# Output rows in falling order: reversed through device memory, two tiles stored from another queue, and a last pair in another order (attention with an FNet mixing block, one Trainium2 core)

## The chip, the cores and the metric

The kernel runs on one core of a Trainium2 chip. The metric is the device time of one execution in microseconds. Three runs of the kernel before gave 1046.66, 1045.99 and 1046.56 us, a median of 1046.56. One further execution was recorded by the hardware profiler; all rows below come from it.

The engines have short names in the profile: PE is TensorE's matmul, PEld its weight load, DVE is VectorE, ACT is ScalarE, POOL is GpSimd, SP is SyncE. SP computes nothing here; it issues DMAs. SPq and ACTq are the queues in which SP and ScalarE issue them. An engine issues its instructions strictly in order, so a DMA that has to wait holds up everything behind it on the same engine.

## The reference

Four batches of 768 rows with 8 heads of 64 columns. A blocked-sparse attention first, then a Fourier mixing over rows and columns, a normalization, and a two-layer multiplication with a residual:

```python
# q, k, v: (4, 8, 768, 64); mask: window of blocks, first and last block, 3 sampled blocks per row block
scores = scale * np.matmul(q, k.transpose(0, 1, 3, 2))
scores = np.where(mask, scores, -1000000000.0)
attn = softmax(scores)                        # with 1e-9 added to the sum
x = np.matmul(attn, v).transpose(0, 2, 1, 3).reshape(4, 768, 512)

mixed = np.real(np.fft.fft(np.fft.fft(x, axis=1), axis=2))
u = x + mixed
un = (u - mean(u)) / np.sqrt(var(u) + 1e-06)  # over the 512 columns
out = u + np.maximum(un @ w_ch1, 0.0) @ w_ch2 # w_ch1: 512x2048, w_ch2: 2048x512
```

The output is `out`, 4 x 768 x 512 in float32.

## The kernel before, in words

**Attention.** The 32 pairs of heads and batches are worked off in slots; a slot holds a few units of scores. `s` (L583) is the matmul of scores, ScalarE and VectorE make `e` from it (L603 or L611 and L613), `o` (L657) multiplies it with the values. At the end of a pair the result `oT` is transposed by TensorE (`xt`, L680) and copied by ScalarE into the activations of its batch (`x<-xt`, L681). For some pairs of the later batches the way goes through device memory instead (`row<-oT`, L696, and `x<-row`, L700).

**The activations.** A batch has two tiles in SBUF, `xA` and `xB`, of 128 partitions x 3 x 512: six tiles of 128 rows, numbered 0 to 5. Each of the two names has two buffers, so a batch uses the buffers of the batch two before it: the first `x<-xt` of a batch waits until every output store of the batch two before has read that buffer.

**The mixer** of a batch runs beside the attention of the batch after it: a list of small steps (Fourier folds, normalization `un`, the channel layers) that a planner places into the slots. The planner keeps a modelled time for each engine (`busy`), and steps have due times. The list of matmuls is thereby fixed when the kernel is built. The normalized rows `un` of some tiles go to device memory (`far<-un`, L1020) and come back transposed (`unT<-far`, `fetch`, L1032: four DMAs for each half); the matmuls `xp`, `yp` and `z` of L1116 need them, `z` after a subtraction on VectorE (`t`, L1070). Both kinds are issued by SP.

**The output.** `channels` (L1270) makes `y` (L1281: a tile of the first layer times a chunk of `w_ch2`) and adds it to `x` in place (L1284). In the last round of a tile `store` (L1289) sends it to the output, all on SP's queue. In the first three batches the tiles of half 0 come in the order 2, 0, 1, and those of half 1 in the order 3, 4, 5. In the last batch, where no attention is left to run beside it, tiles m and m + 3 are made as a pair, with products and sums of blocks (`outputs`, `product` L1349, `plus` L1356), in the order m = 0, 1, 2; the last pair stores its four halves of 256 columns as each is done, one of them from ScalarE's queue.

**Which rows a tile holds.** The Fourier symmetry makes partitions correspond to rows in an unusual order, listed in `_ORDER` and turned into access patterns by `_rows`. Tiles 0 and 1 hold even and odd rows in two runs of 64: two DMAs of `64x512`. In tiles 2, 3 and 4 the rows *fall*: partitions 1 to 126 hold two interleaved runs of 63 descending rows, which a DMA writes with the pattern `[[row, 2], [-2 row, 63], [1, 512]]` (a `2x63x512` in what follows), and partitions 0 and 127 hold one row each, with a DMA of their own. Tile 5 has rising rows in four runs of 1, 48, 15 and 64 rows.

**Completions.** A DMA's end is counted by a semaphore. The DMAs of SP and ScalarE use eight of these in rotation, and a DMA waits until the one eight before it has landed.

**Loads on the same queue.** The blocks of k and q (`kb`, `qb`, L232) and v (`vr`, L272) of later pairs are also issued by SP.

These are the functions that the change touches, and those that call them:

Of the kernel before, what the change touches and what calls it, by code (L numbers as in the profile page):

```python
# [11 lines left out]
FP32 = mybir.dt.float32  # L12
# [5 lines left out]
ALU = mybir.AluOpType  # L18
ACT = mybir.ActivationFunctionType
# [61 lines left out]
def _rows(view, tile):  # L81

    got = []
    for t, p0, runs, jump, n, s0, step in _ORDER:
        if t != tile:
            continue
        at = view[s0:s0 + 1, :]
        row, col = list(at.ap[0])[0], list(at.ap[1])
        if jump > 0 > step:
            got.append((p0, runs * n, bass.AP(tensor=at.tensor, offset=at.offset,  # L90
                                              ap=[[jump * row, runs], [step * row, n], col])))
            continue
        for r in range(runs):
            at = view[s0 + r * jump:s0 + r * jump + 1, :]
            got.append((p0 + r * n, n, bass.AP(tensor=at.tensor, offset=at.offset,
                                               ap=[[step * row, n], col])))
    return got
# [3 lines left out]
def kernel(  # L101
# [14 lines left out]
    nc = tc.nc  # L116

    B, H, S, D = q.shape
    DM = H * D
    FF = w_ch1.shape[1]  # L120
    P = 128
# [9 lines left out]
    T = C // 2  # L131
# [55 lines left out]
    far_p = ctx.enter_context(tc.tile_pool(name="far_p", bufs=1, space=bass.MemoryType.DRAM))  # L187
    ps_s = ctx.enter_context(tc.tile_pool(name="ps_s", bufs=2, space=PSUM))
    ps_o = ctx.enter_context(tc.tile_pool(name="ps_o", bufs=1, space=PSUM))
    ps_t = ctx.enter_context(tc.tile_pool(name="ps_t", bufs=1, space=PSUM))  # L190
    ps_m = ctx.enter_context(tc.tile_pool(name="ps_m", bufs=2, space=PSUM))
# [3 lines left out]
    when = {"PE": 0.0, "ACT": 0.0, "DVE": 0.0, "POOL": 0.0}  # L195
    free = {"m": [0.0, 0.0], "t": [0.0]}

    def busy(engine, us, after=0.0):
        when[engine] = max(when[engine], after) + us
        return when[engine]  # L200
# [101 lines left out]
    def bit(n):  # L302
# [5 lines left out]
                      in_=bass.AP(tensor=_words(sampled_blocks, NB * NR), offset=0,  # L308
                                  ap=[[0, NB], [1, 2 * NB * NR]]))
# [138 lines left out]
    for w, w_sb in ((w_ch1, w1_sb), (w_ch2, w2_sb)):  # L448
        rows, cols = w.shape
        words = _words(w, rows * cols)  # L450
        for row in range(rows // P):
            for col in range(0, cols, WN):
                src = bass.AP(tensor=words, offset=2 * (row * P * cols + col),
                              ap=[[2 * cols, P], [1, 2 * WN]])
# [527 lines left out]
    z_at = [0.0, 0.0]  # L982
    rstd_at = deque()
    finished = set()
    folded = set()

    def mixer(b, xA, xB):
# [4 lines left out]
        tt = nc.vector.tensor_tensor  # L992
# [51 lines left out]
        t, s = {}, {}  # L1044
# [243 lines left out]

        def store(half, m, cols=slice(0, DM), queue=nc.sync):  # L1289
            x = (xA, xB)[half]  # L1290
            for p0, cnt, rows in _rows(out[b][:, cols], T * half + m):
                queue.dma_start(out=rows, in_=x[p0:p0 + cnt, m, cols])
            if cols.stop == DM:
                stored[half] += 1
            if stored[half] == T:
                finished.add((b, half))

        stored = [0, 0]
        last = b == B - 1
        OUT = (0, 1, 2) if last else (2, 0, 1)
        out_of = (OUT, OUT if last else (0, 1, 2))
        o_t, o_s = {}, {}
        DH = DM // 2

        def block(r, k, n):
            return w2_sb[:, 8 * r + 4 * k:8 * r + 4 * k + 4, n * DH:n * DH + DH]
# [25 lines left out]
        def outputs(r, m, after):  # L1335

            if m == OUT[0]:
                output_left(m, 1)
                output_left(m, 2)
            a11, a12, a21, a22 = (hs[g, i][:, :, m * P:(m + 1) * P]  # L1340
                                  for i in range(2) for g in range(2))
            a0, a1 = xA[:, m, 0:DH], xA[:, m, DH:DM]
            b0, b1 = xB[:, m, 0:DH], xB[:, m, DH:DM]
            rights = {j: [o_t[j, 0], o_t[j, 1]] for j in (1, 2, 3, 4)}

            def product(pool, tag, a, c):
                ps = pool.tile([P, 512], FP32, tag=tag, name="yy")[:, 0:DH]
                for k in range(4):
                    nc.tensor.matmul(ps, a[:, k, :],  # L1349
                                     c[k // 2][:, k % 2, :] if isinstance(c, list) else c[:, k, :],  # L1350
                                     start=(k == 0), stop=(k == 3))
                busy("PE", 1.75)
                return ps

            def plus(to, a, c=None):
                tt(out=to, in0=a, in1=to if c is None else c, op=ALU.add)  # L1356
                busy("DVE", 0.43)

            def ahead(j):
                if after is not None:  # L1360
                    output_left(after, j)

            ends = r == 1 and after is None
            u = sum_p.tile([P, DH], FP32, tag="oT", name="u")
            p1 = product(ps_m, "m", a11, block(r, 0, 0))
            nc.scalar.copy(out=u, in_=p1)
            plus(a0, p1)
            plus(a0, product(ps_m, "m", a12, block(r, 1, 0)))
            if ends:
                store(0, m, slice(0, DH))  # L1370
            if m == OUT[0]:
                output_left(m, 3)
                output_left(m, 4)
            plus(u, product(ps_t, "t", a21, rights[2]), u)
            plus(a1, u)
            plus(b0, product(ps_s, "s", a22, rights[4]))
            plus(u, product(ps_s, "s", o_s[m, 3], rights[3]), u)
            both = xB[:, m, :].rearrange("p (n d) -> p n d", n=2)
            tt(out=both, in0=both,
               in1=u.rearrange("p (o d) -> p o d", o=1).broadcast_to([P, 2, DH]), op=ALU.add)  # L1380
            busy("DVE", 0.7)


            if ends:
                store(1, m, slice(0, DH), nc.scalar)
            p5 = product(ps_o, "o", o_s[m, 1], rights[1])
            plus(b1, p5)
            if r == 1:
                store(1, m, slice(DH if ends else 0, DM))
            plus(a1, p5)  # L1390
            ahead(1)
            ahead(2)
            ahead(3)
            p3 = product(ps_m, "m", o_s[m, 4], block(r, 1, 1))
            plus(a1, p3)
            if r == 1:
                store(0, m, slice(DH if ends else 0, DM))
            ahead(4)

        fl = [[("tm"[h == 1 and m != 0], lambda h=h, m=m: un_flip(h, m), 0.6, 0.55, 0.0)  # L1400
# [10 lines left out]
              for m, us in (((1, 2), RIGHT), ((0,), COMBINE))]  # L1411
        le = [("d", lambda i=i: left(0, i), 0.0, 0.0, COMBINE) for i in (1, 3, 4)]
        after = ([fl[0][1], sp[1][1]] + le +
                 [fl[0][2], sp[1][2], wh[1][1], fl[0][0], sp[1][0], wh[1][2],
                  fl[1][1], fl[1][2], wh[1][0]] + ri[0] + [fl[1][0]] + ri[1])
        if not last:
# [5 lines left out]
            after = ([("-", un_back, 0.0, 0.0, 0.0)] + le +  # L1422
                     [("b", lambda i=i: right(i, 0, 1, 2), 0.0, 0.0, 1.0 if b else 1.7)
                      for i in (1, 2, 3, 4)])
# [5 lines left out]
        for r in range(0 if last else NF // 4):  # L1430
# [21 lines left out]
    needed = set()  # L1452
    state = {"paired": False, "total": None, "w": 0, "got": 0, "owed": 0.0, "ready": 0.0,
             "back": 0.0, "place": None,
             "alone": False, "drain": lambda: None}

    def channel_step():
        masks["by_pe"] = False
# [62 lines left out]
    def until(met, alone=False):  # L1521

        state["alone"] = alone
        while not met():
            if late:
                channel_step()
                soon = state.pop("soon", None)
                gap(2.0, start=soon)
            else:
                do_apart()  # L1530
        state["alone"] = False
# [24 lines left out]
    def w_loads():  # L1556
        while state["got"] < min(len(wchunks), state["w"] + len(W_ROOMS)):
            w_load(state["got"])
            state["got"] += 1

    def w_steps(sl):
        while state["w"] < min(len(wchunks), W_PACE * sl):
            w_round(state["w"])
            state["w"] += 1

    def slot(sl):
        phase, r = divmod(sl, SB)
        n, s = divmod(sl, SP)
        units = range(SLOT * sl, SLOT * sl + SLOT)
# [55 lines left out]
        if s >= ((4 if late else 5) if reuse else 3) and (n, 0) in oT_at and once(n):  # L1625
            b, j = pairs[n]
            at = oT_at[n, 0]
# [12 lines left out]
        if sl < B * SB and n % NP == 1 and s == 1:  # L1640
            b = pairs[n - 1][0]
            at = oT_at[n - 1, 1]
            if b >= 2:
                until(lambda: (b - 2, 1) in finished)
                at = when["PE"] + LEAVES
# [46 lines left out]
        while short and (not more or soon) and (  # L1692
# [5 lines left out]
            short.remove(item)  # L1698
            item[2]()
        w_loads()  # L1700
        w_steps(sl)
        table_step(sl)

# [32 lines left out]
    begin(B - 1)  # L1736
    state["drain"] = lambda: None
    until(lambda: len(finished) == 2 * B, True)
    ordered.close()

    def general():
# [4 lines left out]
        for b in range(B):  # L1748
            xs = [xp.tile([P, T, DM], FP32, tag=tag, name="x") for tag in ("xA", "xB")]
            for h in range(H):  # L1750
                qt = ld.tile([P, C, 2, D], FP32, tag="q", name="qg")
                for t in range(C):
                    for p0, cnt, rows in _rows(q[b, h], t):
                        nc.sync.dma_start(out=qt[p0:p0 + cnt, t, 0, :], in_=rows)
                nc.sync.dma_start(out=qt[:, :, 1, :],
                                  in_=k[b, h].rearrange("(p c) d -> p c d", p=P))
                vt = ldv.tile([P, C, D], FP32, tag="v", name="vg")
                nc.sync.dma_start(out=vt, in_=v[b, h].rearrange("(p c) d -> p c d", p=P))
                for half in range(2):
# [4 lines left out]
                    sl = slice(half * HS, (half + 1) * HS)  # L1764
# [3 lines left out]
                op = ps_o.tile([P, C, D], FP32, tag="o", name="og")  # L1768
# [32 lines left out]
                step[1]()  # L1801
            for fn, _ in rest:
                fn()

    with tc.If(over > 0):
        general()
# [37 lines left out]
```

## Time and profile before

| | us |
|---|---|
| median of three runs | 1046.56 |
| the profiled execution | 1045.29 |
| its span, first to last instruction | 1043.6 |
| TensorE (PE) busy | 1018.6 |
| VectorE busy | 683.2 |
| ScalarE busy | 359.3 |
| mean granted TensorE clock, of full speed | 0.994 |
| last matmul begins | 1035.48 |
| last sum (DVE, L1356) ends | 1035.92 |
| last output store lands | 1041.70 |

The profiled execution's time stands 1.7 us over its span. A row such as `653.32 2.93 PE L583 MATMUL s<-qT,kT 64*128 64x384 f32 x8 [4.52 <-DVE e L613]` is read thus: from 653.32 us after the span's start, for 2.93 us, PE ran eight matmuls of line 583; it had been idle for 4.52 us before, and what ended that idle time was VectorE's `e` of line 613. For a row of SPq or ACTq the second number is the time in which the queue issued the DMAs, waits between them included; when their data landed is read from the events of their semaphores, and the number of such events tells on how many DMA engines a transfer ran.

The second batch's half 0 is stored from 633.06 us on, the first batch's from 389.61 on.

### The profile page before, as it was taken

How to read it: one execution, taken by the hardware profiler on the slowest of the kernel's cores; microseconds unless marked ns; L12 is line 12 of the kernel's file. 1: busy time of each engine (PE TensorE's matmuls, PEld its weight loads, DVE VectorE, ACT ScalarE, POOL GpSimd, SP SyncE). 2: the span in 40 equal slices, each digit the busy share in tenths (PEclk: the TensorE clock that was granted, in tenths of full speed). 3: DMA queues.
4: the chain of work that ended last, by engine and by line, in shares of the span. 5: the costliest groups of instructions: out<-in, count | busy, mean ns of one | idle time of the engine just before them, and what ended most of it. 6: DMA issues, size and time to landing. Idle time of an engine off the chain costs nothing.

```text
span 1043.6 us, 12498 instructions
## 1 busy us (share of the span) xinstructions
PE 1018.6 (98%) x4382; PEld 537.0 (51%) x4382; DVE 683.2 (65%) x1246; ACT 359.3 (34%) x727; POOL 257.7 (25%) x287
## 2 busy tenths in 40 slices
PE   8999999999999999999999998999999999999996
PEld 4444345435565454444535653444444764578575
DVE  6899895978745646655677367665458475674663
ACT  6998765563021012433341111253220221210210
POOL 1000173662000203545560003256540221000000
PEclk9999999999999999999999999899999999999998
DMA  7767422291000143322320005521010001000001
GB/s 213 225 190 234 99 47 46 51 153 25 1 1 20 41 58 65 73 47 45 63 46 1 1 20 101 91 48 43 17 23 8 0 1 42 20 0 1 1 19 45
DMA packets 163582, 58.06 MB, mean 56 GB/s; under 512 B 144298, under 2 KB 154296, under 8 KB 163512
## 3 DMA queue, kind: packets, MB, share of 16 engines
q1 hardware_dynamic: 162216, 56.46, 24.1%
q10 hardware_dynamic: 1264, 0.72, 0.3%
q8 instruction: 36, 0.59, 0.2%
q14 instruction: 34, 0.28, 0.1%
q0 software_dynamic: 32, 0.01, 0.0%
HBM read 43.80 MB, written 13.37 MB: 55 GB/s over the span
## 4 chain that ended last, share of the span: by engine, by line
PE 84%; DVE 8%; DMA 2%; ACT 2%; SPq 2%; issue 1%; ACTq 0%; DVEq 0%
PE y L1281 20%; PE z L1116 16%; PE s L583 11%; PE o L657 9%; PE yp L1116 8%; PE yy L1349 7%; PE xp L1116 4%; PE zp L865 2%; PE sp L728 1%; PE s L593 1%; DMA far<-un 1%; ACT e L603 1%; DVE t L1070 1%; PE yz L1224 1%; DVE acc L638 1%
## 5 line engine op out<-in xcount | busy, mean ns | idle before, releaser
L643 POOL TENSOR_TENSOR acc<-acc,e 128x384 f32<-128x384 f32 x160 | 163.4, 1054 | 126.3 <-DVE e L613 106.7
L583 PE MATMUL s<-qT,kT 64*128 64x384 f32 x768 | 154.5, 518 | 9.5 <-DVE e L613 5.4
L657 PE MATMUL o<-e,vr 128*64 128x384 f32 x768 | 141.7, 497 | 0.0
L1281 PE MATMUL y<-w_sb,hB 128*128 128x512 f32 x264 | 118.9, 601 | 0.0
L1281 PE MATMUL y<-w_sb,hA 128*128 128x512 f32 x264 | 117.1, 595 | 0.0
L613 DVE TENSOR_TENSOR e<-s,mask 128x768 f32<-128x768 f32 x86 | 78.3, 950 | 53.9 <-ACT s L611 45.9
L583 PEld LDWEIGHTS s<-qT,kT 64*128 64x128 f32 x768 | 64.4, 187 | 90.0 <-ACT e L603 22.7
L1284 DVE TENSOR_TENSOR x<-y,x 128x512 f32<-128x512 f32 x66 | 45.6, 691 | 98.3 <-PE y L1281 98.1
L611 ACT ACTIVATE s<-s 128x768 f32<-128x768 f32 x86 | 65.1, 791 | 107.3 <-PE s L583 107.2
L603 ACT ACTIVATE e<-s 128x768 f32<-128x768 f32 x106 | 81.0, 814 | 54.2 <-PE s L593 32.9
L643 POOL TENSOR_TENSOR acc<-e 128x384 f32<-128x384 f32 x42 | 48.7, 1180 | 201.5 <-ACT e L603 121.9
L1116 PE MATMUL z<-unT,t 128*128 128x384 f32 x256 | 93.1, 486 | 0.0
L657 PEld LDWEIGHTS o<-e,vr 128*64 128x64 f32 x768 | 47.9, 136 | 69.4 <-issue 67.0
L1281 PEld LDWEIGHTS y<-w_sb,hB 128*128 128x128 f32 x264 | 49.6, 192 | 62.0 <-issue 61.3
L1121 DVE TENSOR_TENSOR hA<-z,hA 128x384 f32<-128x384 f32 x64 | 35.7, 557 | 69.8 <-PE z L1116 69.7
L1281 PEld LDWEIGHTS y<-w_sb,hA 128*128 128x128 f32 x264 | 49.2, 190 | 59.5 <-issue 55.7
L1125 ACT ACTIVATE hA<-hA 128x384 f32<-128x384 f32 x64 | 33.5, 523 | 121.8 <-DVE hA L1121 121.8
L1116 PEld LDWEIGHTS z<-unT,t 128*128 128x128 f32 x256 | 48.6, 190 | 34.1 <-DVE hA L1121 0.4
L1125 ACT ACTIVATE hB<-hB 128x384 f32<-128x384 f32 x64 | 33.5, 523 | 86.0 <-DVE hB L1121 86.0
L1136 ACT COPY hA<-xp 128x384 f32<-128x384 f32 x32 | 15.3, 477 | 129.3 <-PE xp L1116 129.3
L1116 PE MATMUL z<-t,w_sb 128*128 128x384 f32 x128 | 46.7, 487 | 1.5 <-DVE t L1070 1.5
L1116 PE MATMUL xp<-unT,w_sb 128*128 128x384 f32 x128 | 47.2, 492 | 0.0
(236 smaller groups left out, 1440.4 us busy)
## 6 DMA issues: line engine op xcount, KB each, us to landing
wraw<-in_moe_w_ch_dram SPq DMA_DIRECT2D x32, 512.0 KB
vr<-in_v_dram SPq DMA_DIRECT2D x30, 192.0 KB
far<-un SPq DMA_DIRECT2D x18, 256.0 KB
unT<-far SPq DMA_DIRECT2D x24, 192.0 KB
qb<-in_q_dram SPq DMA_DIRECT2D x44, 96.0 KB
kb<-in_k_dram SPq DMA_DIRECT2D x44, 96.0 KB
out_dram<-x SPq DMA_DIRECT2D x11, 252.0 KB
out_dram<-x SPq DMA_DIRECT2D x19, 128.0 KB
```

Source lines behind the costliest of these rows:

```text
L583: nc.tensor.matmul(s[:, i, 0:HS], kT[rows, c * P:(c + 1) * P], qT[rows, queries], start=True, stop=u not in by_pe)
L603: nc.scalar.activation(out=e, in_=s[:, :, 0:HS], func=ACT.Exp, scale=scale)
L611: nc.scalar.activation(out=s[:, :, 0:HS], in_=s[:, :, 0:HS], func=ACT.Exp, scale=scale)
L613: nc.vector.tensor_tensor(out=e, in0=s[:, :, 0:HS], in1=m.broadcast_to([P, 2, HS]), op=ALU.mult)
L643: nc.gpsimd.tensor_add(out=acc[:, i, :], in0=start[:, i, :], in1=e[:, i, :])
L657: nc.tensor.matmul(o[D * i:D * i + D, :], vt[:, i, c, :], e[:, i, :], start=(c == 0), stop=(c == C - 1))
L1116: nc.tensor.matmul(to, a[:, k, :], c[:, k, :], start=(k == 0), stop=(k == ND // 2 - 1))
L1121: tt(out=to, in0=ps, in1=a, op=ALU.add)
L1125: nc.scalar.activation(out=h, in_=h, func=ACT.Relu)
L1281: nc.tensor.matmul(y, hs[0, half][:, l, m * P:(m + 1) * P], w2_sb[:, 4 * r + l, :], start=(l == 0), stop=(l == 3))
L1284: nc.vector.tensor_tensor(out=x[:, m, :], in0=y, in1=x[:, m, :], op=ALU.add)
L1349: nc.tensor.matmul(ps, a[:, k, :], c[k // 2][:, k % 2, :] if isinstance(c, list) else c[:, k, :], start=(k == 0), stop=(k == 3))
```

## The change

1. **Falling tiles through device memory.** In the first three batches a falling tile is no longer written to the output in descending rows. `turn_round` writes it in ascending order into a tile in device memory (`falls`): one DMA `falls<-x` with the pattern `[[512, 2], [1024, 64], [1, 512]]` from all 128 partitions, and for tile 2 one row more. When the falling tiles of a half are there, `fall` copies them from device memory to the output, with descending rows: one DMA `out<-falls`, `[[256, 2], [-512, 128], [1, 256]]` for half 0 (tile 2, 256 KB), `[[256, 2], [-512, 256], [1, 256]]` for half 1 (tiles 3 and 4 and a row of tile 5, 512 KB). All are on SP's queue. A fall is noted in `owed` and issued ahead of the next store, or at the end of a later slot; on SP it waits until the `falls<-x` of its half have landed. In half 0 the next store is that of tile 0, so the fall stands ahead of tiles 0 and 1.
2. **Two tiles from ScalarE.** Tiles 0 and 1 of the second and third batch (`0 < b < B - 1`) are stored by ScalarE's queue, four DMAs of `64x512` for a batch.
3. **The last pair.** The last batch's order is m = 2, 0, 1, so that the last pair is tiles 1 and 4. Its last step has its products in another order: both halves of the falling tile 4 are finished first and stored from ScalarE's queue (still in descending rows), those of tile 1 last, from SP's.

In the program that results, TensorE, VectorE and GpSimd have as many instructions as before, and in the same order up to the last pair of the last batch. ScalarE issues ten DMAs more.

```diff
@@ -982,6 +982,7 @@
     z_at = [0.0, 0.0]
     rstd_at = deque()
     finished = set()
+    owed = deque()
     folded = set()
 
     def mixer(b, xA, xB):
@@ -1288,19 +1289,57 @@
 
         def store(half, m, cols=slice(0, DM), queue=nc.sync):
             x = (xA, xB)[half]
-            for p0, cnt, rows in _rows(out[b][:, cols], T * half + m):
+            if half == 0 and m != T - 1 and 0 < b < B - 1:
+                queue = nc.scalar
+                busy("ACT", 1.1, when["DVE"])
+            while owed:
+                owed.popleft()[1]()
+            falls = T * half + m in (T - 1, T, T + 1) and not last
+            if falls:
+                turn_round(half, m)
+            for p0, cnt, rows in sorted(_rows(out[b][:, cols], T * half + m), key=lambda i: -i[1]):
+                if falls and (cnt > 1 or p0 or m):
+                    continue
+                if not last and half == 1 and m == T - 1 and cnt == 1:
+                    rows = falling[1][2 * P:2 * P + 1, :]
                 queue.dma_start(out=rows, in_=x[p0:p0 + cnt, m, cols])
-            if cols.stop == DM:
-                stored[half] += 1
-            if stored[half] == T:
+            if not last and m == T - 1:
+                owed.append((state["slot"], lambda: fall(half)))
+            stored[half] += cols.stop - cols.start
+            if stored[half] == T * DM:
                 finished.add((b, half))
 
 
 
+
+        falling = {}
+
+        def turn_round(half, m):
+
+            if half not in falling:
+                falling[half] = far_p.tile([(1 + half) * P + 1, DM], FP32, tag=f"fall{half}",
+                                           name="falls", bufs=2)
+            rows = falling[half]
+            x = (xA, xB)[half][:, m, :]
+            at = rows[m * half * P:m * half * P + 1, :]
+            nc.sync.dma_start(out=bass.AP(tensor=at.tensor, offset=at.offset,
+                                          ap=[[DM, 2], [2 * DM, P // 2], [1, DM]]), in_=x)
+            if half == 0:
+                nc.sync.dma_start(out=rows[P:P + 1, :], in_=x[0:1, :])
+
+        def fall(half):
+
+            n = (1 + half) * P
+            src, to = falling[half][1:2, :], out[b][S // 2 * (1 + half) - 1:S // 2 * (1 + half), :]
+            nc.sync.dma_start(
+                out=bass.AP(tensor=to.tensor, offset=to.offset,
+                            ap=[[DM // 2, 2], [-DM, n], [1, DM // 2]]),
+                in_=bass.AP(tensor=src.tensor, offset=src.offset,
+                            ap=[[DM // 2, 2], [DM, n], [1, DM // 2]]))
 
         stored = [0, 0]
         last = b == B - 1
-        OUT = (0, 1, 2) if last else (2, 0, 1)
+        OUT = (2, 0, 1)
         out_of = (OUT, OUT if last else (0, 1, 2))
         o_t, o_s = {}, {}
         DH = DM // 2
@@ -1360,14 +1399,30 @@
                 if after is not None:
                     output_left(after, j)
 
-            ends = r == 1 and after is None
             u = sum_p.tile([P, DH], FP32, tag="oT", name="u")
+            both = xB[:, m, :].rearrange("p (n d) -> p n d", n=2)
             p1 = product(ps_m, "m", a11, block(r, 0, 0))
             nc.scalar.copy(out=u, in_=p1)
             plus(a0, p1)
+            if r == 1 and after is None:
+                plus(u, product(ps_t, "t", a21, rights[2]), u)
+                plus(a1, u)
+                plus(u, product(ps_s, "s", o_s[m, 3], rights[3]), u)
+                tt(out=both, in0=both,
+                   in1=u.rearrange("p (o d) -> p o d", o=1).broadcast_to([P, 2, DH]), op=ALU.add)
+                busy("DVE", 0.7)
+                plus(b0, product(ps_s, "s", a22, rights[4]))
+                store(1, m, slice(0, DH), nc.scalar)
+                p5 = product(ps_o, "o", o_s[m, 1], rights[1])
+                plus(b1, p5)
+                store(1, m, slice(DH, DM), nc.scalar)
+                plus(a1, p5)
+                plus(a1, product(ps_m, "m", o_s[m, 4], block(r, 1, 1)))
+                store(0, m, slice(DH, DM))
+                plus(a0, product(ps_m, "m", a12, block(r, 1, 0)))
+                store(0, m, slice(0, DH))
+                return
             plus(a0, product(ps_m, "m", a12, block(r, 1, 0)))
-            if ends:
-                store(0, m, slice(0, DH))
             if m == OUT[0]:
                 output_left(m, 3)
                 output_left(m, 4)
@@ -1375,18 +1430,13 @@
             plus(a1, u)
             plus(b0, product(ps_s, "s", a22, rights[4]))
             plus(u, product(ps_s, "s", o_s[m, 3], rights[3]), u)
-            both = xB[:, m, :].rearrange("p (n d) -> p n d", n=2)
             tt(out=both, in0=both,
                in1=u.rearrange("p (o d) -> p o d", o=1).broadcast_to([P, 2, DH]), op=ALU.add)
             busy("DVE", 0.7)
-
-
-            if ends:
-                store(1, m, slice(0, DH), nc.scalar)
             p5 = product(ps_o, "o", o_s[m, 1], rights[1])
             plus(b1, p5)
             if r == 1:
-                store(1, m, slice(DH if ends else 0, DM))
+                store(1, m)
             plus(a1, p5)
             ahead(1)
             ahead(2)
@@ -1394,7 +1444,7 @@
             p3 = product(ps_m, "m", o_s[m, 4], block(r, 1, 1))
             plus(a1, p3)
             if r == 1:
-                store(0, m, slice(DH if ends else 0, DM))
+                store(0, m)
             ahead(4)
 
         fl = [[("tm"[h == 1 and m != 0], lambda h=h, m=m: un_flip(h, m), 0.6, 0.55, 0.0)
@@ -1452,7 +1502,7 @@
     needed = set()
     state = {"paired": False, "total": None, "w": 0, "got": 0, "owed": 0.0, "ready": 0.0,
              "back": 0.0, "place": None,
-             "alone": False, "drain": lambda: None}
+             "slot": 0, "alone": False, "drain": lambda: None}
 
     def channel_step():
         masks["by_pe"] = False
@@ -1564,6 +1614,7 @@
             state["w"] += 1
 
     def slot(sl):
+        state["slot"] = sl
         phase, r = divmod(sl, SB)
         n, s = divmod(sl, SP)
         units = range(SLOT * sl, SLOT * sl + SLOT)
@@ -1698,6 +1749,8 @@
             short.remove(item)
             item[2]()
         w_loads()
+        while owed and owed[0][0] < sl:
+            owed.popleft()[1]()
         w_steps(sl)
         table_step(sl)
 
@@ -1736,6 +1789,7 @@
     begin(B - 1)
     state["drain"] = lambda: None
     until(lambda: len(finished) == 2 * B, True)
+    assert not owed
     ordered.close()
 
 
@@ -1801,6 +1855,8 @@
                 step[1]()
             for fn, _ in rest:
                 fn()
+            while owed:
+                owed.popleft()[1]()
 
     with tc.If(over > 0):
         general()
```

## The prediction

> **What bounds the kernel now.** I read the page's first part and its chain first: is any engine but TensorE worth looking at?
>
> ```profile
> PE 1018.6 (98%) x4382; PEld 537.0 (51%) x4382; DVE 683.2 (65%) x1246; ACT 359.3 (34%) x727; POOL 257.7 (25%) x287
> ...
> PE 84%; DVE 8%; DMA 2%; ACT 2%; SPq 2%; issue 1%; ACTq 0%; DVEq 0%
> ```
>
> It isn't. The change leaves every matmul in the program, so it can only move TensorE's few idle stretches, its clock after them, and what follows the last matmul. I looked for idle stretches near output stores. The timeline of PE at the end of the second batch has the largest:
>
> ```profile
> 646.00 2.80 PE L657 MATMUL o<-e,vr 128*64 128x384 f32 x16
> 653.32 2.93 PE L583 MATMUL s<-qT,kT 64*128 64x384 f32 x8 [4.52 <-DVE e L613]
> 656.18 5.15 PE L1281 MATMUL y<-w_sb,hB 128*128 128x512 f32 x8
> ...
> 669.63 1.53 PE L1116 MATMUL z<-t,w_sb 128*128 128x384 f32 x4 [1.30 <-DVE t L1070]
> ```
>
> PE is idle for 4.52 us. Then eight `s` take 2.93 us and eight `y` 5.15, where the same rows ahead of the gap have 1.56 and 3.60: another 2.92 us, with a granted clock of 0.5 for 6.8 us in the records. So the place costs 7.4 us. The timeline of ScalarE names what ended last:
>
> ```profile
> 650.26 0.48 ACT L681 COPY x<-xt 128x384 f32<-128x384 f32 x1 [8.70 <-DMA far<-un]
> ```
>
> This copy fills the `x` buffer of a batch two later, so it waits until the old tiles are stored. It names `far<-un`, but that had landed at 643.23; the trace's completions put tile 1's two stores at 649.69 and 650.01, just ahead of 650.26. The tile was ready at 639.9. SP's queue shows why it left so late:
>
> ```profile
> 633.06 1.53 SPq L1292 DMA_DIRECT2D out_dram<-x  x3
> 635.09 0.35 SPq L1020 DMA_DIRECT2D far<-un  x1
> 636.49 1.19 SPq L1292 DMA_DIRECT2D out_dram<-x  x2
> 637.79 0.53 SPq L1020 DMA_DIRECT2D far<-un  x1
> 641.98 3.96 SPq L1032 DMA_DIRECT2D unT<-far  x4
> 645.98 1.94 SPq L1292 DMA_DIRECT2D out_dram<-x  x2
> 648.02 1.03 SPq L1020 DMA_DIRECT2D far<-un  x2
> 651.38 3.93 SPq L1032 DMA_DIRECT2D unT<-far  x4
> ```
>
> SP works in order. The falling tile 2 (633.06) has a `2x63x512` store; its completions come from two DMA engines only, 7.9 us after its issue at 633.38. A `64x512` store completes on sixteen, 2.7 to 3.7 us after issue when none of those is ahead. Every other DMA has a share on those two engines, so `far<-un` lands at 641.92 instead of some 638 (2.6 us after issue, as the one at 648.66), the fetch waits for it until 641.98, and tile 1 waits behind the fetch.
>
> The end of the first batch has the same stores, and here the wait is harmless:
>
> ```profile
> 400.00 0.48 ACT L681 COPY x<-xt 128x384 f32<-128x384 f32 x1 [1.90 <-DMA out_dram<-x]
> ```
> ```profile
> 402.55 2.80 PE L657 MATMUL o<-e,vr 128*64 128x384 f32 x16
> 405.27 1.56 PE L583 MATMUL s<-qT,kT 64*128 64x384 f32 x8
> ```
>
> PE runs on without a gap. The copy leads PE's `s` by 653.32 − 650.26 = 3.06 us in the second batch, so in the first it could start at 402.2 at the latest.
>
> **The change, part by part.** Sums are against the profiled execution (1045.29 us, span 1043.6); the median shown, 1046.56, is 1.27 more.
>
> *Tiles 0 and 1 of the second and third batch from ScalarE.* Four stores leave as their tiles are ready (636.5 to 641.0) and land at about 643; the copy at L681 starts near 643.3 and the 7.4 us go: **−7.4**. ScalarE issues four DMAs at some 0.55 us; the two exponentials at 640.07 come up to 1 us later, hidden by `y` and `s` up to 646.0 (without that cover: +1). At the end of the third batch no instruction waits for these stores: 0.
>
> *Two transfers for one.* The turning store is `2x64x512` with the 2 outermost, like the old one: two engines, 7.9 us. Then `falls`, DRAM to DRAM, goes to the output as `2x128x256`, again with the 2 outermost. Its price isn't in this trace. The nearest row is the last falling half, `2x63x256`: issued 1036.34, landed 1041.70, so 5.36 us with 63 packets of 1 KB an engine at 46 ns, 2.46 fixed. 128 packets give 2.46 + 5.9 = 8.4 us. The dear end is the 150 ns seen for 2 KB packets in the crowded part, halved: 75 ns, 12.1 us. The cheap end is all sixteen engines: 2.46 + 16 × 0.046 = 3.2. I take 50 ns, 8.9 us, since two completions is what every pattern with a leading 2 shows here.
>
> [...]
>
> *Where it stands on SP.* The fall waits on SP for the turn to land, and whatever SP has next stands behind.
>
> First batch: these tiles 0 and 1 stay on SP. Turn issued 389.6, landed 397.5; fall issued 397.7, landed 406.6. The four tile stores, issued meanwhile, have a share on the two engines and land 0.3 us apart behind it, as they do now (398.74 to 399.71): the last at 407.9. L681 then starts at 408.2 instead of 400.0, PE's `s` at 411.3 instead of 405.3: 6.0 idle. At the half clock that followed 4.52 us: **+8.9**. At 46 ns +8.4; at 75 ns +12.1.
>
> [...]
>
> Second batch: the fall waits on SP from 636.5 to 641.2 and lands at 650.1. Behind it are a `far<-un`, the first fetch, whose third DMA reuses the fall's completion semaphore (8 in rotation) and so starts at 650.2, two `far<-un` (about 652, landing about 656) and the second fetch, from 657 instead of 651.38. It takes 8.3 us from first issue to last landing (651.38 to 659.66): 665.4. `t` at L1070 needs it and now starts at 666.39, 3.24 ahead of `z`. With 7.4 us saved PE would ask for `z` at 662.2; it gets it at 668.7. So only 669.6 − 668.7 = 0.9 of the 7.4 stays, and the gap of over 6 us costs 2.9 in clock: net **+2.0** in place of −7.4. At 46 ns +1.5, at 75 ns +5.2.
>
> Falls of tiles 3 to 5 (512 KB, 256 packets an engine, 14 to 21 us): behind them are `kb`, `vr` and `qb`; `qb` issued at 428.48 and 680.26 is used at 448.5 and 700.3, `kb` at 437.6 and 689, so 10 us or more are to spare: 0. If the cover is gone, a few us each. Third batch: 0, since nothing late reads behind it.
>
> *The end.*
>
> ```profile
> 1034.88 2.66 SPq L1292 DMA_DIRECT2D out_dram<-x  x5
> 1035.50 0.42 DVE L1356 TENSOR_TENSOR x<-yy,x 128x256 f32<-128x256 f32 x1 [0.97 <-PE yy L1349]
> ```
>
> The last sum is done at 1035.92; its falling half lands at 1041.70. In the new order the last half is of tile 1, two `64x256` of sixteen engines, some 3 us after issue at 1036.3 with the falling half ahead of them on ScalarE's queue, begun two products (3.5 us) sooner: about 1039.5. **−2.2**; if the falling halves still end last, −1.
>
> Sum: +8.9 + 2.0 − 2.2 = **+8.7**: 1054.0 on the profiled execution, 1055 on the median.
>
> **The rivals.**
>
> *The fall is quick* (the other side): both transfers' packets spread, or the engines serve them faster. In the first batch the copy has 2.2 us to spare, so it decides whether the fall lands within 3 us of its issue; at 3.2 the loss is 0.1. In the second, fetches stay about where they are and second-fetch data at 659.7 takes 0.7 of the 7.4: −6.7. With −2.2: −8.9, **1037.7**. For it: a `64x512` lands within 3.7 us. Against it: the leading 2.
>
> *One place is covered*: the first batch loses (+8.9) and the second keeps its gain, since the fetches run before the fall's packets: −7.4; or the first is covered and the second pays (+2.0). With −2.2 that is about −0.5, **1046**. For it: fourteen engines are free all the time. Against it: each store and fetch needs all its completions.
>
> *Packets of DRAM to DRAM are dear*: 75 ns, as where the queue is crowded: +12.1 + 5.2 − 2.2 = +15.1, **1061.7**. For it: each is read and written in DRAM. Against it: the 46 ns row.
>
> **How the numbers follow.** Forecast 0.54, quick fall 0.20, one place covered 0.11, dear packets 0.15. The likeliest case alone is 1050 (half clock missed at both places) to 1058. The range reaches to the quick fall, 1037, and to the dear one, 1062. Under about 0.2% (2.1 us) a measurement of this kernel can't tell a change from none. Faster 0.22, same 0.08, slower 0.70.
>
> **What would show it.** Two completions for `falls<-x` and `out<-falls`, the latter 8 to 9 us after issue; L681 near 408 in the first batch with a PE gap of 6 us ahead of `s`; L681 near 643 in the second with no gap there, but one of 6 to 7 us ahead of `z` (or `xp`) near 662; span end some 2 us nearer to the last sum. Sixteen completions, or a first batch without a gap, would make the prediction wrong.

## The result and the profile after

The changed kernel is slower: 1060.83 us median (1059.48 to 1061.56, four runs) beside 1046.34 for the kernel before, a ratio of 1.0137 with a 95% interval of 1.012 to 1.0155. The profiled execution took 1061.56 us with a span of 1059.8; before it was 1045.29 and 1043.6.

The page's first part and its chain first: TensorE has a little more busy time (1018.6 before), by stretches at a lower clock (0.989 granted on the mean, 0.994 before), and a smaller share of a longer span.

```profile
PE 1021.7 (96%) x4382; PEld 538.6 (51%) x4382; DVE 682.2 (64%) x1246; ACT 359.9 (34%) x727; POOL 257.3 (24%) x287
...
PE 84%; DVE 8%; ACT 3%; DMA 2%; issue 1%; SPq 1%; ACTq 0%; DVEq 0%
```

**End of the first batch.** The timeline of PE, of ScalarE and of SP in the changed kernel, in this order:

```profile
403.00 2.80 PE L657 MATMUL o<-e,vr 128*64 128x384 f32 x16
411.74 2.93 PE L583 MATMUL s<-qT,kT 64*128 64x384 f32 x8 [5.94 <-DVE e L613]
...
419.84 0.85 PE L742 MATMUL sp<-acc,pick 128*32 128x384 f32 x8
```
```profile
408.63 0.48 ACT L681 COPY x<-xt 128x384 f32<-128x384 f32 x1 [10.06 <-DMA out_dram<-x]
```
```profile
390.19 0.77 SPq L1325 DMA_DIRECT2D falls<-x  x1
391.01 0.87 SPq L1328 DMA_DIRECT2D falls<-x  x1
398.54 0.68 SPq L1334 DMA_DIRECT2D out_dram<-falls  x1
399.31 3.49 SPq L1305 DMA_DIRECT2D out_dram<-x  x4
```

Read from below: SP stands still from 391.9 to 398.54 because the fall needs the turn, which landed at 398.30 and 398.47. The fall landed at 407.02, with completions of two engines, at 406.64 and 407.02 (its semaphore has one event more, at 399.63, 0.4 us after SP had issued it; from 400.2 to 401.4, when it runs alone, the DMA share is 0.12, two of sixteen). The four tile stores behind it have sixteen events each; of the first one's, fourteen came at 402.43 to 402.67, the last two at 406.97 and 407.34. The four landed at 407.34 to 408.32; the copy starts at 408.63, and PE's `s`, which followed `o` without a gap before, now comes after 5.94 us of idle time and at half clock (2.93 us; the records have a granted clock of 0.5 from 411.04 to 417.87).

**End of the second batch.** The same three timelines:

```profile
659.11 1.78 PE L583 MATMUL s<-qT,kT 64*128 64x384 f32 x8 [0.59 <-DVE e L613]
...
676.63 2.90 PE L1117 MATMUL z<-t,w_sb 128*128 128x384 f32 x4 [5.11 <-DVE t L1071]
679.32 2.14 PE L1117 MATMUL z<-t,t 128*128 128x384 f32 x4
...
697.55 1.56 PE L1117 MATMUL xp<-unT,w_sb 128*128 128x384 f32 x4
```
```profile
652.62 0.48 ACT L681 COPY x<-xt 128x384 f32<-128x384 f32 x1 [0.57 <-DMA out_dram<-x]
```
```profile
651.07 0.67 SPq L1334 DMA_DIRECT2D out_dram<-falls  x1
651.79 1.40 SPq L1021 DMA_DIRECT2D far<-un  x1
653.37 7.89 SPq L1033 DMA_DIRECT2D unT<-far  x4
661.36 1.62 SPq L1021 DMA_DIRECT2D far<-un  x2
666.08 4.05 SPq L1033 DMA_DIRECT2D unT<-far  x4
```

ScalarE's stores do what they were to do: the copy waits 0.57 us, and the old gap of 4.52 us is 0.59. But the second fetch now starts 15 us behind the fall and lands at 674.41, and a gap of 5.11 us stands ahead of `z`.

**The end.** A view of what SP waited for from 1020 us on, and the last rows of SP and VectorE:

```profile
SPq L1305 <- DMA out_dram<-x: 26.1, 3, 21.7
```
```profile
1044.48 0.42 DVE L1395 TENSOR_TENSOR x<-yy,x 128x256 f32<-128x256 f32 x1 [1.30 <-PE yy L1388]
1044.95 10.07 SPq L1305 DMA_DIRECT2D out_dram<-x  x9
```

One wait of 21.7 us, for another output store. SP had issued tile 2's row at 1022.93; its next DMA, tile 3's `2x63x512`, left at 1044.95. The tile had been ready since 1031.1. In the program this DMA's completion semaphore is the one that ScalarE's first half of tile 4 has; that store was issued at 1039.76 and landed at 1044.89, 0.06 us before. So nine stores of tiles 3, 0 and 1 leave after the last sum. The last two, of tile 1's last half, have another wait: the first of them has the semaphore of tile 3's `2x63x512`, stands from 1050.16 on and leaves at 1053.92, when that store has landed (1053.86). The last landing is at 1056.54, 11.6 us after the last sum (5.8 before).

By place, from the times of the same rows in both traces. The `sp` and `xp` of before are

```profile
410.40 0.85 PE L742 MATMUL sp<-acc,pick 128*32 128x384 f32 x8
...
688.53 1.56 PE L1116 MATMUL xp<-unT,w_sb 128*128 128x384 f32 x4
```

and those of the changed kernel stand above at 419.84 and 697.55.

| | forecast | profiled execution | from |
|---|---|---|---|
| until the first batch's end | 0 | +0.4 | `s` 395.65 → 396.10 |
| end of the first batch | +8.9 | +9.0 | `sp` L742 410.40 → 419.84 |
| end of the second | +2.0 | −0.4 | `s` 639.10 → 648.55, `xp` 688.53 → 697.55 |
| third batch, order of the last | 0 | 0.0 | last sum ends 1035.92 → 1044.90 |
| from the last sum to the end of the span | −2.2 | +7.2 | 7.7 → 14.9 |

### The profile page after: what moved, and what is told of

It is laid out like the page before. It is cut to its first block, busy times and chain, and to the rows that moved or that the text cites. A ratio compares the mean times of both kernels' runs of the same rounds, so it can differ in the third digit from the quotient of the medians.

```text
span 1059.8 us, 12488 instructions
## 1 busy us (share of the span) xinstructions
PE 1021.7 (96%) x4382; PEld 538.6 (51%) x4382; DVE 682.2 (64%) x1246; ACT 359.9 (34%) x727; POOL 257.3 (24%) x287
## 2 busy tenths in 40 slices
DMA packets 165876, 60.43 MB, mean 57 GB/s; under 512 B 144282, under 2 KB 156584, under 8 KB 165806
## 4 chain that ended last, share of the span: by engine, by line
PE 84%; DVE 8%; ACT 3%; DMA 2%; issue 1%; SPq 1%; ACTq 0%; DVEq 0%
PE y L1282 20%; PE z L1117 16%; PE s L583 11%; PE o L657 9%; PE yp L1117 8%; PE yy L1388 7%; PE xp L1117 4%; PE zp L865 2%; PE sp L728 1%; PE s L593 1%; ACT e L603 1%; PE yz L1225 1%; DVE e L613 1%; DVE acc L638 1%; DVE t L1071 1%
```

## Experiments

All medians in us; the kernel before ran beside each (1045.8 to 1046.0). Under "The parts alone" a measured difference is against the kernel before, in the section after it against the changed kernel (1060.83).

| run | median | runs | ratio to before |
|---|---|---|---|
| scalar_stores_alone | 1040.37 | 5 | 0.9943 [0.9929, 0.9956] |
| last_pair_alone | 1044.25 | 11 | 0.9985 [0.9976, 0.9994] |
| old_last_pair | 1056.49 | 4 | 1.0104 [1.0088, 1.0119] |
| tile4_from_sp | 1053.08 | 4 | 1.0061 [1.0046, 1.0077] |
| fall_in_sixteen | 1041.29 | 4 | 0.9958 [0.9943, 0.9973] |
| fall_behind_tiles | 1047.70 | 9 | 1.0021 [1.0011, 1.003] |
| no_falls_rest | 1038.46 | 5 | 0.9933 [0.992, 0.9947] |
| no_falls_tile4_from_sp | 1037.71 | 5 | 0.9922 [0.9908, 0.9935] |
| fall_behind_tile4_sp | 1039.00 | 4 | 0.9940 [0.9923, 0.9958] |

The theory after the traces: the fall's place on SP costs 9 us in the first batch and takes back what ScalarE's stores gain in the second, because it runs on two engines and everything behind it has a share on these; at the end SP waits for a completion semaphore that it shares with ScalarE. The rivals: the bytes or the two engines of the falls cost by themselves, wherever they stand; and at the end, the falling halves of tile 4 crowd the two engines.

### The parts alone

**scalar_stores_alone**, the kernel before with

```diff
             x = (xA, xB)[half]
+            if half == 0 and m != T - 1 and 0 < b < B - 1:
+                queue = nc.scalar
+                busy("ACT", 1.1, when["DVE"])
```

> The kernel before with one part of the change: tiles 0 and 1 of the second and third batch stored by ScalarE. No falls, old last pair. Theory: the gap of 4.52 us at the end of the second batch and the half clock behind it go, -7.4 less up to 1: about 1039 to 1040. Rival (the fetch, not the store, sets this place): the gap moves to the ahead of z, and the time stays within 2 us of 1046.

Measured −5.6. The copy waits 0.31 us, and `z` keeps its old gap of 1.30, so the store and not the fetch set this place. It is 1.8 less than the place had cost, of which 1.1 are new small gaps at the two `s` of that place:

```profile
644.61 1.78 PE L583 MATMUL s<-qT,kT 64*128 64x384 f32 x8 [0.49 <-DVE e L613]
649.72 1.78 PE L583 MATMUL s<-qT,kT 64*128 64x384 f32 x8 [0.59 <-DVE e L613]
```

ScalarE is late there; its exponentials begin at 642.13 (640.07 before):

```profile
642.13 1.50 ACT L611 ACTIVATE s<-s 128x768 f32<-128x768 f32 x2 [12.57 <-DMA out_dram<-x]
643.94 0.48 ACT L681 COPY x<-xt 128x384 f32<-128x384 f32 x1 [0.31 <-DMA out_dram<-x]
```

Its fourth store stood from 639.95 to 641.61 for the completion semaphore of SP's falling store of tile 2, which landed at 641.59. So one queue waits for a DMA of the other through the shared semaphores without any fall, too.

Part of the rest is clock. In the profiled execution the granted clock is 0.5 from 883.69 to 887.11, in the third batch, and the eight matmuls of `xp` and `yp` there take 1.7 us longer than the same ones before:

```profile
881.46 0.66 PE L1001 MATMUL utp<-ident,un 128*128 128x128 f32 x4 [1.16 <-DVE un L960]
882.85 0.63 PE L1001 MATMUL utp<-ident,un 128*128 128x128 f32 x4 [0.73 <-ACT unT L1002]
883.31 2.39 PE L1116 MATMUL xp<-unT,w_sb 128*128 128x384 f32 x4
```

The kernel before has the same two gaps (1.16 and 0.73 us, at 887.66 and 889.05) at full clock. Of the eleven profiles here, old_last_pair and tile4_from_sp have such a stretch of 3.4 us at this place as well, the other eight none.

**last_pair_alone**, the changed kernel with `falls = False` and without ScalarE's stores of tiles 0 and 1. It keeps one more thing of the change: `store` issues the pieces of a tile with the most rows first.

> The kernel before with the new order of the last batch alone: pairs 2, 0, 1, tile 4's halves from ScalarE, tile 1's from SP at the end. No falls, no other store from ScalarE. Theory: what goes wrong at the end of the changed kernel is that the rotation of the eight completion semaphores there gives SP's store of tile 3 the semaphore of ScalarE's store of tile 4, so SP waits 14 us with tile 3 in hand; without falls the rotation comes out in order (SP's stores of tile 3 behind SP's of tile 2), and the last landing comes some 3.6 us after the last sum instead of 11.6: about -2, 1044. Rival: it is the falling halves of tile 4 that crowd the two engines; then the last landing stays 10 us or more behind the last sum here too, and the time is about 1052.

Measured −1.8: the last landing is 4.8 us after the last sum. Tile 3's store was issued at 1021.75, right when it was ready, and ScalarE's falling halves are all there. The crowding rival falls; what undoes the new last pair in the changed kernel is its meeting with the falls.

### The changed kernel with one thing undone

**old_last_pair**: the last batch as before.

> The changed kernel with the last batch of the kernel before. Theory: the loss at the end (11.6 instead of 5.8 us from last sum to last landing, and 1.4 more to the end of the span) goes, the other two stay: 1060.8 - 7.2 = about 1053.5. Rival (the loss at the end comes from late falls, not from the order of the last pair): no change, 1060.

Measured −4.3, less than expected. The last landing is 8.2 us after the last sum, not 5.8: with falls in the program ScalarE's four stores of tile 5 are numbered ahead of and between SP's two of tile 1 here too. SP waits 4.7 us with tile 1's second store for its own falling store of tile 4, which is eight before it in that numbering (landed 1038.40), and 4.1 us with a row of tile 2 for a store of ScalarE's (landed 1044.30). SP's falling last half left at 1047.08, the last landing was 1052.48. The waits are only shorter.

**tile4_from_sp**:

```diff
-                store(1, m, slice(0, DH), nc.scalar)
+                store(1, m, slice(0, DH))
...
-                store(1, m, slice(DH, DM), nc.scalar)
+                store(1, m, slice(DH, DM))
```

> The changed kernel with tile 4's halves stored by SP instead of ScalarE, nothing else. All stores of the last batch are then in SP's order and no one waits for a DMA of ScalarE. Theory: tile 3's store leaves when its tile is ready, near 1032, the last landing comes 4 to 5 us after the last sum: about 1054. Rival (crowding by the falling halves): they still come just ahead of tile 1's on the same two engines, and now on the same queue, so it gains nothing: 1060 or more.

Measured −7.8, with SP's waits for other stores from 1005 us on down to one:

```profile
SPq L1305 <- DMA out_dram<-x: 0.5, 1, 0.5
```

Tile 3's store left at 1032.17, the last landing came 4.0 us after the last sum, with the same bytes on the same two engines. So the loss at the end is SP's wait for ScalarE's completion. From the last sum to the end of the span the profile has 5.9 us instead of 14.9; 1.1 of these 9.0 are lost again before the last sum, where this execution has 3.4 us at half clock from 898.79 on.

**fall_in_sixteen**:

```diff
-                            ap=[[DM // 2, 2], [-DM, n], [1, DM // 2]]),
+                            ap=[[DM // 16, 16], [-DM, n], [1, DM // 16]]),
...
-                            ap=[[DM // 2, 2], [DM, n], [1, DM // 2]]))
+                            ap=[[DM // 16, 16], [DM, n], [1, DM // 16]]))
```

> The changed kernel with the fall's pattern led by 16 column pieces of 128 bytes instead of 2 of 1 KB; bytes, place on SP and waits are the same. Theory (two engines are what makes the fall long): sixteen completions, the fall lands 3.5 to 5 us after its issue instead of 8.5; the first batch's copy at L681 starts near 404 instead of 408.6 and PE's gap there is 1 to 2 us instead of 5.9, with no half clock: about 6 us less there; in the second batch the fetch is 4 to 5 us earlier and most of the 5.1 us gap ahead of z goes; the rotation of completion semaphores comes out in order at the end: 6 less. Together about 1060.8 - 6 - 5 - 6 = 1044. Rival (a transfer from device memory to device memory is slow by its bytes or its small pieces, whatever the engines): fall no shorter than 8 us, gaps as before, 1054 from the end alone.

Measured −19.5. The fall has sixteen completions and lands 3.7 us after its issue (398.57 to 402.26; 644.31 to 648.02; 5.1 us in the third batch), in pieces of 128 bytes, eight times smaller. The two gaps of PE, from its timeline in this run:

```profile
407.74 1.78 PE L583 MATMUL s<-qT,kT 64*128 64x384 f32 x8 [1.83 <-DVE e L613]
```
```profile
666.35 1.53 PE L1117 MATMUL z<-t,w_sb 128*128 128x384 f32 x4 [1.58 <-DVE t L1071]
```

At the end the semaphores come out in order: the last landing is 5.1 us after the last sum. So it is the two engines that make the fall long, and not its being from device memory to device memory: an engine has 128 packets in both kernels, of 1 KB with two engines (46 ns each in the trace) and of 128 bytes with sixteen (13 ns). 128-byte pieces on two engines were not run. The time alone doesn't part the end from the rest; the profile does: 8.1 us less from the last sum to the end of the span, 12.3 less before it.

**fall_behind_tiles**:

```diff
-            while owed:
+            while owed and half:
                 owed.popleft()[1]()
```

> The changed kernel with the fall of tile 2 issued by SP later: not ahead of the stores of tiles 0 and 1, but ahead of the next half's or at the end of a later slot. The same transfers, two engines each. Theory (its place on SP is what costs, in the first two batches): no gap of 6 us in the first batch, -8.9; in the second the fetches run ahead of it, no gap of 5 us ahead of z, about -6. The end stays as in the changed kernel. 1060.8 - 15 = about 1046. Rival (the turn with its two engines is enough to hold these tiles): the copy at L681 still starts after 402.2 in the first batch and a gap stays.

Measured −13.1. The first batch has no gap, with the same two-engine fall behind the tiles (398.10 to 406.96); the copy starts at 399.45:

```profile
404.94 1.56 PE L583 MATMUL s<-qT,kT 64*128 64x384 f32 x8
```

The second batch's `z` is back at a gap of 1.30. The end is as in the changed kernel:

```profile
SPq L1305 <- DMA out_dram<-x: 26.1, 3, 21.7
```

### What can be kept

**no_falls_rest**: the changed kernel with `falls = False` (the pieces of a tile again with the most rows first).

> The kernel before with both parts that gained alone: tiles 0 and 1 of the second and third batch from ScalarE, and the new last pair; falling tiles stored directly as before. Theory: the two gains add, 1046.0 - 5.6 - 1.8 = about 1038.6. Rival (they share something, the rotation of completion semaphores for one): the end is at 7 us or more behind the last sum again, and the time is 1040 or more.

1038.46: the two gains add. **no_falls_tile4_from_sp** is this with the edit of tile4_from_sp.

> As the run with both parts that gained, with tile 4's halves from SP instead of ScalarE. The changed kernel with that edit had its last landing 4.0 us after the last sum, the last pair alone with ScalarE 4.8. Theory: 0.8 us less than with ScalarE, about 1037.8, which five rounds may or may not tell apart. Rival: the two queues side by side are better, 1039 or more.

1037.71, the fastest; its profile has 3.9 us from the last sum to the last landing, the one with ScalarE 5.2. This kernel is 8.1 us faster than the kernel before and 23 faster than the changed one.

**fall_behind_tile4_sp**: the changed kernel with the edits of fall_behind_tiles and tile4_from_sp, all falls kept.

> The changed kernel with both places mended and all falls kept: the fall of tile 2 issued behind the stores of tiles 0 and 1, and tile 4's halves stored by SP. Theory (the whole loss is the fall's place on SP in the first two batches, and SP's wait at the end for a completion semaphore that ScalarE's store holds): 1047.7 - 8 = about 1039.5, within 2 us of the kernel with both gains and no falls (1037.7). Rival (falls cost more of their own, by the extra 2.3 MB or the two engines): 1043 or more.

1039.00. With both places mended, the falls with their two engines and their extra traffic (60.43 MB by the page instead of 58.06) cost 1.3 us by the medians of this run and of the fastest, which did not run beside each other; the four executions here spread over 2.6 us, so the size is uncertain.

## Why the prediction was right, and where it was wrong

**Slower: right, and by the forecast mechanism in the first two places, not at the end.** The range held the time, but the sum was too small: +8.7 forecast against +14.5 by the medians and +16.3 in the profiled executions. That the range held it is luck: 1060.8 lies above the 1050 to 1058 of the likeliest case, and the range went up to 1062 only for dear packets, which these are not. The 1050 has the half clock missed at both places, the author's estimate; no run shows that. In the changed kernel the granted clock was 0.5 for 6.8 us at both, with idle stretches of 5.94 and 5.11 us.

*The first batch* (+8.9, measured +9.0): right in each step. Turn 8.1 us after issue, fall 8.5 (forecast 8.9, at 50 ns a packet; its 1 KB packets took 46 ns, as in the row of the last falling half); copy at 408.63 (408.2); idle 5.94 (6.0); half clock after it (0.5 granted up to 417.87). The experiments show the two conditions apart: sixteen engines leave 1.83 us of idle time, and another place on SP none.

*The number of engines.* The forecast took two completions for the fall, 8.9 us, and not the cheap end of sixteen, 3.2. The runs have it so, for a transfer from device memory to device memory too: two late completions, the last 8.5 us after issue, with a 2 outermost (the changed kernel), and sixteen, the last 3.7 us after issue, with a 16 (fall_in_sixteen). No other outermost dimension was run for the fall.

*The second batch* (+2.0, measured −0.4): right in mechanism. The second fetch was 665.4 in the forecast, and 674.41 less the 9.45 that the place begins later is 665.0. What was off is the clock: the half-speed stretch cost 2.1 us (`z` 2.90 and 2.14 us where 1.53 and 1.45 were before), not 2.9, because the granted clock was 0.5 from 673.86 to 680.69 and PE stood idle up to 676.63 of it. And 2.4 of the 7.4 had stayed instead of 0.9, since `z` began 2.2 us after the data had landed, not 3.2, and the data came 0.4 sooner than forecast. (The 662.2 at which the forecast has PE ask for `z` leaves out the 1.30 us for which PE was idle ahead of that row; no term changes by it.) Of what holds the first fetch, and with it all that follows on SP, the larger part is the two engines: its first two DMAs, issued at 653.37 and 654.04 and not waiting for the fall's semaphore, landed at 661.13 and 662.29, 2 to 3 us after the fall; SP waited for the fall's semaphore itself for 1.1 us.

*The end* (−2.2, measured +7.2): wrong. The step that failed is "in the new order the last half is of tile 1, two `64x256` of sixteen engines, some 3 us after issue at 1036.3". It priced the stores of the last pair by themselves, and took SP to be free at that time. The landing itself was right, 2.1 us after issue; but these two left at 1053.92 and 1054.43, 9.0 us and more after the last sum, not 0.4. Two things stood against it: SP has to be past tiles 3 and 0 by then, and the eight completion semaphores are handed out in one order over both queues. In the changed program this order has five of ScalarE's six stores of tile 4, which leave from 1039.76 on, ahead of SP's first store of tile 3, which was ready at 1031.1, and SP waits. The last pair alone gives −1.8 by the medians; in its profile the end is 0.8 us nearer to the last sum (6.9 us after 7.7), and the last landing is 4.8 us behind that sum where the forecast had 3.6. So the −2.2 was right in direction for the part and rather too large; the parts together are not the sum of the parts. That the numbering is out of order with the long falls and in order with fall_in_sixteen is seen in the semaphore numbers of the traces; why it is so stays open.

The rival "quick fall" was rightly priced in kind (fall_in_sixteen is 1041.3 with 1.8 and 1.6 us gaps, forecast 1037.7), but it was not this kernel. "Dear packets" has the nearest time, 1061.7, by a mechanism that isn't there: the fall's packets took 46 ns, what the row said, and not 75.

Still open: from the last landing to the end of the span there are 3.3 and 3.2 us in the two kernels with SP's long wait (1056.54 to 1059.8, and 1041.92 to 1045.1 in fall_behind_tiles), 1.9 before.

## What to carry to other kernels

A change of several parts is to be priced at the seams, too. Here two queues share eight completion semaphores, and where the numbering of their DMAs was not their order in time, one waited for the other: SP 21.7 us for a store of ScalarE's at the end of the changed kernel, ScalarE 1.7 us for one of SP's in scalar_stores_alone. The waits of the built program show that. The fall, confined to two engines, was not made cheap by the fourteen that were free: the tile stores issued behind it had their last completions at 407.34 to 408.32, behind its 407.02, though the first of them had fourteen of its sixteen by 402.67. So such a transfer is better put behind whatever has a reader that waits (−13.1 us in fall_behind_tiles), or its outermost dimension made larger, even at the price of far smaller pieces (−19.5 us in fall_in_sixteen, with 128 bytes instead of 1 KB).

## What the runs showed of the hardware

256 KB from device memory to device memory took 8.0 to 9.2 us on two engines in pieces of 1 KB (the three falls of tile 2 in the changed kernel) and 3.7 to 5.1 us on sixteen in pieces of 128 bytes (fall_in_sixteen). A wait of 21.7 us for a completion that belongs to another queue is shown under the name of the store alone; the name of the queue isn't in the row. The half clock, 6.8 us of it each time, came with idle stretches of TensorE of 4.52 us (before), 5.11 and 5.94 us (the changed kernel); single ones of 1.30 to 1.83 us were not followed by it. But no single stretch decides: two of 1.16 and 0.73 us, with only short matmuls between them, were followed by 3.4 us at half clock in three profiles (883.69 to 887.11 in scalar_stores_alone) and by none in the other eight.
